# A planned instruction order in which the transfers of one in-order queue wait longer for what they depend on

## The chip, the core and the metric

The kernel runs on one core of one Trainium2 chip. A core has a matrix engine (PE), a vector engine (DVE), an activation engine (ACT), a general engine (POOL) and a synchronising engine (SP), which here issues every transfer. The metric is the device time of one execution in microseconds, as the median of several runs.

## What is computed

A pre-LayerNorm transformer block on 2048 rows of 640 values: multi-head attention with 32 heads of 20 values each, and then a gated feed-forward part without a nonlinearity. All tensors are bf16.

```python
def _A_ref(x, wqkv, wo):
    qkv = (x @ wqkv).reshape(B, S, 3, H, Dh).transpose(2, 0, 3, 1, 4)
    q, k, v = qkv[0], qkv[1], qkv[2]
    p = softmax(einsum("bhqd,bhkd->bhqk", q, k) * Dh ** -0.5)
    o = einsum("bhqk,bhkd->bhqd", p, v)
    return o.transpose(0, 2, 1, 3).reshape(B, S, D) @ wo

def _B_ref(x, w_gate, w_up, w_down):
    return ((x @ w_gate) * (x @ w_up)) @ w_down

h = x + _A_ref(layernorm(x), wqkv, wo)
out = h + _B_ref(layernorm(h), w_gate, w_up, w_down)
```

B is 1, S is 2048, D is 640, H is 32, Dh is 20, and the feed-forward width is 1728.

## The kernel before

**A planner writes the order.** The program is not a loop nest. While it is built, an event loop (lines 1587 to 1605) plays the kernel on an imagined chip: every operation has a planned duration (lines 68 to 81), a list of what it depends on and a key for its priority. Whenever an engine is free at the planned time, `try_start` (line 287) takes the ready operation of lowest key and emits its instruction. `finish` (line 241) is called with the planned end of an operation and makes those that depend on it available. What comes out is one fixed list of instructions for each engine. On the chip each engine works through its list in that order, and waits at an instruction until what it needs is there. A planned time is never seen by the chip, only the order that came of it. `SWITCH` (line 64) is the planned pause when PE goes from one way of tiling its array to another (line 502).

**The work.** The queries are cut into five chunks (line 37): three of 512 and two of 256. In each chunk the 32 heads form eight groups of four, so there are 40 groups in all, counted here from 0 to 39. A list `stream` (line 900) names the score blocks in order: chunk, group, head and key block. It has 2048 entries, and `spos` counts how far it is used. A group of the first three chunks has 64 entries, one of the last two has 32.

**Scores and exponentials.** PE writes scores into PSUM (`rows_into`, line 997, matmul at line 1013): three banks SA, two banks SB, and two banks D0 and D1. ACT takes the exponential of a whole SA or SB (line 1088) into the tiles EA or EB. Blocks in the D banks go to DVE, which makes integers that read as bf16 are an approximation of the exponential: line 1113 produces the first of four tiles Y, line 1123 two more on DVE, and line 1121 the fourth on POOL. PE then multiplies each tile by the values (line 1164), and accumulates in the bank ACC. The number of columns of VX includes ones, so that row 20 of each head in ACC is the softmax sum.

**Closing a group.** `close_group` (line 1180) is the chain that the change touches most. DVE copies ACC to SBUF (acs, line 1195). Then come small transfers on SP, all issued through `dma` (line 355, instruction at line 360): the sums go to DRAM (dscr<-acs), come back spread over partitions (dn<-dscr), DVE takes their reciprocal (rn, line 1199), which goes to DRAM (rscr<-rn), and comes back as a broadcast to 128 partitions (bc<-rscr, 256 KB for a chunk of 512 and 128 KB for one of 256). POOL multiplies (os, line 1227), and four or five transfers put the result in the layout of the output projection (ON<-os, line 1232). There are two acs tiles and one bc tile.

**What else is on SP's queue.** `dense` (line 574) projects q and k, and stores them in DRAM (qscr, kscr, line 586), from which they are loaded in the layout that the scores need (KTt, line 685; QT, line 700). There are also the loads of weights and x, the DMA transposes after a LayerNorm (line 477), and the stores of the output (line 887). SP is one queue: a transfer that is not ready holds all that stand behind it.

**Work beside attention.** The projections, the output projection, and the feed-forward part (jobs, `make_job`, line 524) are put by PE in between as it has time, in the D banks. When nothing is to be done and the planner thinks PE would be idle too long, it emits small filler matmuls (line 1472). What is left of the last chunks after attention runs at the end on PE.

Of the kernel before, what the change touches and what calls it, by code (L numbers as in the profile page):

```python
# [59 lines left out]
LAT = 0.12  # L60
LATP = 0.23
LPOOL = 0.1
DMA_LAT = 1.5
SWITCH = 0.105
WINDOW = 3.413


# [4 lines left out]
def c_psum(n):  # L72
    return 0.075 + 1.04e-3 * n
# [73 lines left out]
def kernel(  # L147
# [81 lines left out]
    now = [0.0]  # L229
    lockt = {"DVE": 0.0, "POOL": 0.0}  # L230

    def tick(t):
        heapq.heappush(wake, t)

    def enqueue(op):
        seq[0] += 1
        for e in op.engs:
            heapq.heappush(coming[e], (op.avail, seq[0], op))
        tick(op.avail)

    def finish(op, t, e=None, end=None):

        op.done = t
        for u in op.users:
            u.left -= 1
            if e == "DVE" and isinstance(u, Op) and u.engs == ("POOL",):
                u.avail = max(u.avail, t + LPOOL)
            u.avail = max(u.avail, end if e is not None and isinstance(u, Op) and u.engs == (e,) and e != "SP" else t)
            if u.left == 0:
                if isinstance(u, Op):  # L250
                    enqueue(u)
                else:
                    release_later(u.avail, u.cb)
        op.users = []
        tick(t)

    def add(engs, dur, fn, key, deps=(), **kw):
        if isinstance(engs, str):
            engs = (engs,)
        op = Op(engs, dur, fn, flat(key), deps, **kw)  # L260
        if op.left == 0:
            op.avail = max(op.avail, now[0])
            enqueue(op)
        return op
# [3 lines left out]
    def release_later(t, f):  # L268
        seq[0] += 1
        heapq.heappush(later, (t, seq[0], f))  # L270
        tick(t)

    def after(deps, cb):
        c = Call()
        c.left = 0
        c.avail = now[0]
        c.cb = cb
        for d in deps:
            if d.done is None:
                d.users.append(c)  # L280
                c.left += 1
            else:
                c.avail = max(c.avail, d.done)
        if c.left == 0:
            release_later(c.avail, cb)

    def try_start(e):
# [32 lines left out]
        if got.hook is not None:  # L320
            got.hook(t, end, e)
        got.fn(e)
        finish(got, end + got.lat, e, end)
        tick(end)
        return True


    def copy_on(e, o, i):
        if e == "ACT":
            nc.scalar.copy(o, i)  # L330
        else:
            nc.vector.tensor_copy(o, i)  # L332

    attn = {"started": False, "over": False}
# [20 lines left out]
    def dma(o, i, key, deps=(), dur=0.6, lat=1.25, kb=0):  # L355

        def hook(t, end, e):
            landed[0] = max(landed[0], end + 0.3) + kb / 310.0
            op.lat = max(lat, landed[0] - end + 1.4)
        op = add("SP", dur, lambda e: nc.sync.dma_start(o, i), key, deps, lat=lat, hook=hook)  # L360
        return op

    with tc.manual_schedule():
# [48 lines left out]
        def layer_norm(tiles, key, tdeps, dst_of, tr_key, on_pe, front=False, on_act=False):  # L412
# [37 lines left out]
            def one_done(end):  # L450
                left[0] -= 1
                if left[0] == 0:
                    finish(last, end + 0.3)
# [45 lines left out]
        def pe_issue(mode, grp, dur, w=0.25):  # L499
            t = max(now[0], pe["next"])  # L500
            if mode != pe["mode"]:
                t = max(t, pe["end"] + SWITCH)
                pe["mode"] = mode
# [20 lines left out]
        def make_job(mms, deps, evac, mode="C", front=False):  # L524

            j = Job(mms, list(deps), evac)
            j.out = Mark()
            j.mode = mode
            j.target = tgt[0]
            if front:  # L530
                j.target = -1e9
                jq.appendleft(j)
            else:
                jobs.append(j)
                jq.append(j)
            return j
# [5 lines left out]
        def both():  # L542
            return ("DVE", "ACT") if not attn["started"] or attn["over"] else ("DVE",)
# [30 lines left out]
        def dense(wname, col, w, b, dst):  # L574
            mms = []
            for c in range(KT):
                mms.append((lambda lo, hi, c=c: WQ[:, c, col + lo:col + hi],
                            lambda c=c: LT[:, c, b * 512:(b + 1) * 512], 0, 512, w, c == 0, c == KT - 1, 0.216))
            st = Mark()

            def evac(bank, pm):
                k = qd_n[0] % len(QD)
                qd_n[0] += 1
                deps = [pm] + ([qd_busy[k]] if qd_busy[k] is not None else [])
                ev = add(both(), c_psum(512), lambda e: copy_on(e, QD[k][0:w, :], bank[0:w, :]), EVK, deps)
                d = dma(dst, QD[k][0:w, :], 6, [ev], dur=0.75, kb=w, lat=2.2)
                qd_busy[k] = d
                after([d], lambda: finish(st, now[0]))
                return ev
            make_job(mms, [wl[wname], wl[wname + "0"]] + lt_ops, evac)  # L590
            return st
# [202 lines left out]
        def half_jobs(ci, half, pair, hsl, h_marks):  # L794
# [61 lines left out]
            for i, tt in enumerate(pair):  # L856
                ys = {}
                ym = [Mark(), Mark()]
                for hf in range(2):
# [6 lines left out]
                    def evac(bank, pm, tt=tt, hf=hf, ys=ys, ym=ym):  # L866
# [16 lines left out]
                        def rel():  # L883
                            finish(ym[hf], now[0])
                            if ym[1 - hf].done is not None:
                                row = q0 + tt * P
                                add("SP", 0.6, lambda e: nc.sync.dma_start(out2d[row:row + P, :], ys["t"][1][:]), 900, [],
                                    hook=stored, lat=DMA_LAT)
                        after([op], rel)
# [17 lines left out]
        spos = [0]  # L907
# [272 lines left out]
        def close_group(ci, g, end):  # L1180
# [50 lines left out]
            def out_of(p0, f, m):  # L1231
                return add("SP", 0.75, lambda e: nc.sync.dma_start(ON[f % P:f % P + m, on_of[ci, f // P], 0:cw], o[p0:p0 + m, 0:cw]),
                           (10,), mus, lat=DMA_LAT)
            os_use[k] = [out_of(*p_) for p_ in parts]
# [148 lines left out]
        def c_round(c, late, hold):  # L1383
# [4 lines left out]
            else:  # L1388
                t0 = max(now[0], pe["end"] + SWITCH)
                g = [t0] * 4  # L1390
# [93 lines left out]
        def dry():  # L1484

            return max(free["ACT"], now[0]) + sum(act_q.values())

        def room_for(d):

            t = max(now[0], pe["end"]) + d + (SWITCH if d or pe["mode"] != "R" else 0.0)  # L1490
            return t + SCORE + MARGIN <= dry()
# [145 lines left out]
```

The softmax here doesn't subtract the row's maximum and nothing guards it: scores larger than these inputs give would overflow.

## Time and profile before

| | us |
|---|---|
| median of 5 runs | 858.31 |
| lowest, highest | 853.0, 860.01 |
| the profiled execution: its own time | 858.31 |
| the profiled execution: span, first to last instruction | 856.5 |
| PE busy | 817.1 (95%) |
| ACT busy | 763.4 (89%) |
| DVE busy | 731.0 (85%) |
| POOL busy | 352.4 (41%) |
| mean granted TensorE clock | 0.991 of full speed |

"Busy" is the time in which at least one instruction of the engine runs. PE works on up to four parts of its array at once, so its share says little on how much more it could do. In a row of instructions, the name left of the arrow is written and the name right of it is read, with buffer numbers left out; the idle time in brackets is that of the engine just before the instruction, and after the arrow stands what ended it. SPq rows show the time that SP took to issue a transfer, not the transfer itself.

### The profile page before, as it was taken

What the parts mean: (1) busy time and instruction counts of PE and PEld (TensorE: products, weight loads), DVE (VectorE), ACT (ScalarE), POOL (GpSimd) and SP (SyncE); (2) the same over time, 40 slices, a digit from 0 to 9 for tenths busy, and PEclk for the clock granted to TensorE, in tenths of its full rate; (3) what the DMA queues carried; (4) which work ended last, traced back from release to release, by engine and by line L of the source; (5) the groups of instructions that cost most, each with busy time, mean ns of one, the idle gap of its engine ahead of it and who ended that gap; (6) DMA issues with size and microseconds to landing.
All of it is one profiled execution on the core that took longest, in us unless ns stands there. A gap on an engine that the chain in (4) does not pass through costs nothing. (4 is left out here: it accounts for less than half of the span.)

```text
span 856.5 us, 36007 instructions
## 1 busy us (share of the span) xinstructions
PE 817.1 (95%) x15355; PEld 403.8 (47%) x15355; DVE 731.0 (85%) x1961; ACT 763.4 (89%) x714; POOL 352.4 (41%) x593
## 2 busy tenths in 40 slices
PE   8999999999999999999999999999899999999998
PEld 3433343432333444444334444444555655555776
DVE  7888798887899899998999989898889998999342
ACT  5899899998989999999999999999989999999111
POOL 2034444453454444354554444444454444444100
PEclk9999999999999999999999999999999999999999
DMA  9603322322134412110101011100111111001200
GB/s 297 118 21 123 104 78 80 120 70 80 50 101 118 110 41 43 30 49 29 38 23 34 23 31 46 43 23 28 33 36 37 26 38 42 28 13 37 50 17 16
DMA packets 70545, 49.76 MB, mean 58 GB/s; under 512 B 31792, under 2 KB 66448, under 8 KB 70384
## 3 DMA queue, kind: packets, MB, share of 16 engines
q1 hardware_dynamic: 70384, 47.46, 20.3%
q8 instruction: 120, 1.97, 1.0%
q14 instruction: 41, 0.34, 0.1%
HBM read 30.88 MB, written 10.32 MB: 48 GB/s over the span
## 5 line engine op out<-in xcount | busy, mean ns | idle before, releaser
L1088 ACT ACTIVATE EA<-SA 128x1536 bf16<-128x1536 f32 x321 | 466.4, 1453 | 22.4 <-PE SA L1013 14.0
L1121 POOL TENSOR_SCALAR Y<-Y 128x512 uint16<-128x512 uint16 x452 | 290.5, 643 | 405.8 <-DVE Y L1123 262.5
L1113 DVE TENSOR_SCALAR Y<-D 128x512 uint16<-128x512 f32 x452 | 308.3, 685 | 50.6 <-PE SA L1013 18.6
L1088 ACT ACTIVATE EB<-SB 128x1024 bf16<-128x1024 f32 x319 | 328.7, 1030 | 8.1 <-PE SB L1013 4.8
L1164 PE MATMUL ACC<-Y,VX 128*32 128x512 bf16 (+1 forms) x2284 | 262.3, 340 | 5.6 <-DVE acs L1195 5.0
L1123 DVE TENSOR_SCALAR Y<-Y 128x512 uint16<-128x512 uint16 x904 | 242.8, 314 | 8.3 <-POOL Y L1121 0.5
L1164 PE MATMUL ACC<-EA,VX 128*32 128x512 bf16 (+1 forms) x1196 | 217.0, 341 | 0.0
L1013 PE MATMUL D<-QT,KTt 20*128 20x512 bf16 (+1 forms) x571 | 173.4, 339 | 8.8 <-DVE Y L1113 8.0
L1164 PE MATMUL ACC<-EB,VX 128*32 128x512 bf16 (+1 forms) x793 | 174.4, 342 | 0.0
L1013 PEld LDWEIGHTS <-KTt 20*128 20x128 bf16 x2560 | 72.0, 91 | 206.3 <-issue 197.3
L1347 PEld LDWEIGHTS <-R 128*32 128x32 bf16 x5370 | 123.7, 96 | 91.6 <-issue 74.0
L1164 PEld LDWEIGHTS <-VX 128*32 128x32 bf16 x4273 | 118.5, 96 | 87.1 <-issue 66.1
L1013 PE MATMUL SA<-QT,KTt 20*128 20x512 bf16 (+1 forms) x1196 | 129.5, 342 | 5.2 <-ACT EA L1088 4.0
L1347 PE MATMUL D<-L,R 128*32 128x256 bf16 x3240 | 128.0, 275 | 4.4 <-DVE HH L847 2.5
L1013 PE MATMUL SB<-QT,KTt 20*128 20x512 bf16 (+1 forms) x793 | 127.8, 343 | 1.1 <-ACT EB L1088 1.0
L1347 PE MATMUL D<-R 128*32 128x160 bf16 (+1 forms) x2130 | 106.8, 302 | 3.0 <-DVE KTt L332 0.9
L1227 POOL TENSOR_TENSOR os<-acs,bc 128x128 bf16<-128x128 f32 x128 | 57.1, 474 | 50.4 <-DMA bc<-rscr 30.7
L847 DVE TENSOR_TENSOR HH<-D,gs 128x256 bf16<-128x256 f32 (+1 forms) x103 | 43.6, 423 | 16.0 <-ACT gs L330 13.3
L1347 PE MATMUL D<-R,HH 128*32 128x320 bf16 x1120 | 55.5, 302 | 0.5 <-DVE Y L1113 0.4
L1347 PEld LDWEIGHTS <-HH 128*32 128x32 bf16 x1120 | 27.4, 96 | 20.3 <-issue 15.3
L332 DVE CAST gs<-D 128x256 bf16<-128x256 f32 x84 | 34.8, 415 | 1.5 <-PE D L1347 1.1
L1347 PE MATMUL D<-WO,ON 128*32 128x320 bf16 x560 | 32.4, 303 | 2.3 <-DVE hr L771 2.1
(78 smaller groups left out, 389.6 us busy)
## 6 DMA issues: line engine op xcount, KB each, us to landing
bc<-rscr SPq DMA_DIRECT2D x24, 256.0 KB
KTt<-kscr SPq DMA_DIRECT2D x6, 512.0 KB
QT<-qscr SPq DMA_DIRECT2D x22, 128.0 KB
t<-in_A_x_dram SPq DMA_DIRECT2D x16, 160.0 KB
bc<-rscr SPq DMA_DIRECT2D x16, 128.0 KB
R<-in_B_w_gate_dram SPq DMA_DIRECT2D x4, 480.0 KB
R<-in_B_w_up_dram SPq DMA_DIRECT2D x4, 480.0 KB
ON<-os SPq DMA_DIRECT2D x84, 20.0 KB
```

Of the source, the lines that this page charges most:

```text
L332: nc.vector.tensor_copy(o, i)
L847: mu = add("DVE", c_psum(256), lambda e: nc.vector.tensor_tensor(HH[0:M, f, :], bank[0:M, 256:512], GS[k][0:M, :], ALU.mult), EVK, mdeps)
L1013: nc.tensor.matmul(bank[:, n * cw:(n + 1) * cw], lhsT=KTt[32 * j:32 * j + Dh, g, kt * P:(kt + 1) * P], rhs=QTt[32 * j:32 * j + Dh, g, 0:cw ...
L1088: nc.scalar.activation(st["e"][eslot["i"]][:, 0:n * 512], src[:, 0:n * 512], ACT.Exp, scale=SCALE)
L1113: p_ = add("DVE", c_psum(512), lambda e: nc.vector.tensor_scalar(YT[ys[0]][:, :], bank, scalar1=EXP_A, scalar2=EXP_B, op0=ALU.mult, op1=AL ...
L1121: nc.gpsimd.tensor_scalar(o, i_, scalar1=float(d), scalar2=1.0, op0=ALU.add, op1=ALU.mult)
L1123: nc.vector.tensor_scalar(o, i_, scalar1=float(d), scalar2=None, op0=ALU.add)
L1164: nc.tensor.matmul(ACC[32 * j:32 * j + 32, 0:cw], lhsT=VX[:, kt, h * VS:h * VS + 32], rhs=ap, start=(n == 0), stop=last, tile_position=(0, ...
L1227: mus.append(add("POOL", 0.1 + 2.3e-3 * MUW, lambda e, c0=c0, c1=c1: nc.gpsimd.tensor_tensor(o[:, c0:c1], a[:, c0:c1], BC[0][:, c0:c1], AL ...
L1347: nc.tensor.matmul(bank[32 * j:32 * j + 32, c0:c1], lhsT=lhs(32 * j, 32 * j + 32), rhs=rhs(), start=first, stop=last, tile_position=(0, 32 ...
```

## The change

Three things are added to the planner, and one constant is changed. No instruction's operands or sizes are edited.

- When an operation ends, each SP transfer that depends on it becomes available later: by MSP (0.8 us) where it ended as a transfer of SP, otherwise by MSX (0.3 us). This holds from the start of attention until entry 1850 of 2048 of the stream (NEND), which lies in the second group of the last chunk.
- A store of projected q or k counts as done MQ (0.8 us) later for the loads that read it back.
- SWITCH goes from 0.105 to 0.1038.

```diff
@@ -60,8 +60,12 @@
 LAT = 0.12
 LATP = 0.23
 LPOOL = 0.1
+MSP = 0.8
+MSX = 0.3
+MQ = 0.8
+NEND = 1850
 DMA_LAT = 1.5
-SWITCH = 0.105
+SWITCH = 0.1038
 WINDOW = 3.413
@@ -238,11 +242,16 @@
+    def steady():
+        return attn["started"] and spos[0] < NEND
+
     def finish(op, t, e=None, end=None):
 
         op.done = t
         for u in op.users:
             u.left -= 1
+            if isinstance(u, Op) and u.engs == ("SP",) and steady():
+                u.avail = max(u.avail, t + (MSP if e == "SP" else MSX))
             if e == "DVE" and isinstance(u, Op) and u.engs == ("POOL",):
                 u.avail = max(u.avail, t + LPOOL)
@@ -585,7 +594,7 @@
                 d = dma(dst, QD[k][0:w, :], 6, [ev], dur=0.75, kb=w, lat=2.2)
                 qd_busy[k] = d
-                after([d], lambda: finish(st, now[0]))
+                after([d], lambda: finish(st, now[0] + MQ))
                 return ev
```

## The prediction

> **What bounds the kernel now.** I read the page first, then the engine waits, then the timelines of SP, DVE, PE and ACT around the longest ACT gaps, then busy time by stretch.
>
> ```profile
> PE 817.1 (95%) x15355; PEld 403.8 (47%) x15355; DVE 731.0 (85%) x1961; ACT 763.4 (89%) x714; POOL 352.4 (41%) x593
> L1088 ACT ACTIVATE EA<-SA 128x1536 bf16<-128x1536 f32 x321 | 466.4, 1453 | 22.4 <-PE SA L1013 14.0
> L1088 ACT ACTIVATE EB<-SB 128x1024 bf16<-128x1024 f32 x319 | 328.7, 1030 | 8.1 <-PE SB L1013 4.8
> ```
>
> From 19 to 791 us ACT runs one exponential after another: 466.4 + 328.7 = 795 us by start-to-end, less what overlaps. Back to back a pair EA, EB takes 2.24 us, so the stream paces attention, and an ACT gap is lost time. After 794 us comes a tail in which PE alone works (62 us). In the stretches from 60 to 790 us ACT is busy 704.3 of 730 us: 25.7 us of gaps. Whose are they?
>
> ```profile
> DVE rn L1199 <- DMA dn<-dscr: 7.8, 4, 2.8
> ...
> POOL os L1227 <- DMA bc<-rscr: 30.7, 17, 3.9
> ...
> PE D L1347 <- DMA L<-t: 0.8, 1, 0.8
> ```
>
> Total, number and longest: the reciprocal of the softmax sums (line 1199) is reached by DVE before its sums are back, four times, at 88, 205, 280 and 621 us. The last, followed over the engines (start, duration):
>
> ```profile
> 613.87 0.58 SPq L360 DMA_DIRECT2D bc<-rscr  x1
> 614.55 0.52 SPq L360 DMA_DIRECT2D dscr<-acs  x1
> 620.20 0.32 SPq L360 DMA_DIRECT2D dn<-dscr  x1
> ```
> ```profile
> 621.74 0.20 DVE L1199 RECIPROCAL rn<-dn 128x8 f32<-128x8 f32 x1 [2.81 <-DMA dn<-dscr]
> ```
> ```profile
> 622.56 0.26 PE L1013 MATMUL D<-QT,KTt 20*128 20x256 bf16 x1 [2.26 <-DVE Y L1113]
> ```
> ```profile
> 623.01 1.45 ACT L1088 ACTIVATE EA<-SA 128x1536 bf16<-128x1536 f32 x1 [2.40 <-PE SA L1013]
> ...
> 626.26 1.45 ACT L1088 ACTIVATE EA<-SA 128x1536 bf16<-128x1536 f32 x1 [0.87 <-PE SA L1013]
> ```
> ```profile
> 615.00:620.00 5.00, 4.98 (x126) 3.17 (x114) 3.93 (x12) 5.00 (x6) 1.23 (x2) 1.00 0.19 58
> 620.00:625.00 5.00, 2.74 (x47) 1.38 (x50) 3.26 (x9) 2.60 (x3) 4.28 (x8) 0.81 0.07 12
> 625.00:630.00 5.00, 4.75 (x130) 2.87 (x122) 4.03 (x12) 4.08 (x4) 3.28 (x6) 0.85 0.17 51
> ```
>
> dscr stood 0.1 us behind the 128 KB broadcast bc, so dn could only be issued 5.13 us after dscr's issue ended; DVE stood 2.81 us, the bank D it should have emptied held PE 2.26 us, ACT lost 2.40 + 0.87 us. The seventh column after the range is the granted TensorE clock: it falls to 0.81 and 0.85, the second bill of the same stall. The clock falls also near 91, 207 and 248 us: two of these three again just after such a reciprocal.
>
> **What the Trainium skill says.** "PSUM — Partial Sum Buffer", section "Engine vs sequencer instructions": "ScalarE/VectorE/GpSimdE queues are strict FIFO." The trace agrees: the 2.81 us held all that stood behind the reciprocal. "TensorE: Matmul & The Clock Gate", Part 1 on the clock gate: after an idle window of about 3.4 us the array runs at half clock for such a window. The half-clock stretches agree (about 3.4 us), the cause only in part: here 1.7 to 2.3 us of idle with thin work around it was enough. "DMA: Bandwidth & Descriptors", "Queues, rings and completion order": SP's transfers share one row of rings, consumed in ring order. The trace agrees: dscr to dn takes 1.2 us in quiet groups, and 5.13, 2.41 and 2.46 us where dscr stood 0.1 us behind bc. Same page, "Rules for kernel authors": issue early, wait late; this is what a margin in the plan does for the waiting engine.
>
> **The change part by part.** The profiled execution took 858.31 us (span 856.5 and 1.8 around it), which is also the median of the five runs; the sum is made against it. No operation's form is new; margins and SWITCH alter only when the planner believes things possible, hence the orders. I compared the two built orders. PE's first difference is at row 407, so nearly everything is reshuffled; the counts stay close.
>
> (1) Margins before the reciprocal. dscr's availability moves 0.3 us, dn's another 0.8, so the planner puts the reciprocal later among DVE's work. I summed the DVE work between the copy of line 1195 and the reciprocal in both orders (0.60 us for line 1113, 0.20 for line 1123, others by their rows): in groups 0 to 32 the mean cover rises from 5.7 to 6.9 us. In the four groups with waits, 1, 6, 9 and 24, it rises by 1.2, 1.6, 1.8 and 1.2 us against waits of 1.05, 2.61, 1.28 and 2.81. ACT's gaps after them, by its timeline, are 2.03, 3.31, 0.94 and 3.27: 9.55. Groups 1 and 9 are covered. Group 6 keeps 1.0 of 2.61, or 1.3 of ACT's 3.31. In group 24 bc no longer stands ahead of dscr; what comes in its place is in (6). Saved: 9.55 - 1.3 = 8.3. Bounds: 4 if the new order merely moves half of them, 9.6.
>
> (2) Margins before bc and the products. Between the copy and the os products (line 1227) POOL now has 9.4 instead of 7.5 of its line-1121 operations (mean, groups 0 to 33); at one per 770/452 = 1.7 us that is 3.1 us, against waits of 3.9 at most. Nearly all of the 30.7 us should go. POOL is busy 41%, so this is worth little: it delays a Y that PE wants. Taken 1; bounds 0 and 3 (the gaps of 2.2 us at 248, after a POOL backlog, and some more). SP's stores ON<-os wait 0.3 later in the plan and are queued behind fewer unready transfers; cover: the output projection wants them a chunk later, 0.
>
> (3) Transposes L<-t: 0.3 later; PE's wait of 0.76 cost ACT 1.19 at 654. Taken 0.5; 0 to 1.2.
>
> (4) Stores and loads of q and k through DRAM: 0.8 (MQ) and 0.3. Loads are planned one group or more ahead; that hides it, taken 0. Without that cover a late load would hold scores 1.1 us per load.
>
> (5) Counts. One EA of 1536 becomes 1024 wide and one EB of 512 (0.58) goes: 1.45 - 1.03 + 0.58 = 1.0 saved on ACT; DVE takes two more units, beside ACT. In the tail the change leaves the jobs the same, but the 112 filler matmuls between the projection and the down projection go (one before: 1.68 us on the chain), as three down projections now cover the last LayerNorm instead of one; likewise the 0.5 us wait for L. Saved 2.2 (bounds 0 and 2.8). The other 44 + 112 fillers more stand where the plan has idle PE: 0.
>
> (6) What it adds. In groups 24, 26, 27, 29, 30 and 33 bc of the previous group now stands between dscr and dn; before, only in 38. dn is then the small transfer behind the big one. Behind it wait rscr and the next stores on SP, and DVE at the reciprocal. Nearest row: dscr behind bc, 1.2 to 3.9 us late. Need without that: 0.1 + 0.54 (issue) + 1.2 (landing, which hides bc's 0.6) + 0.33 + 2.15 (dn's landing at 205 and 280 us) = 4.3 us; two transposes ahead in 27 and two loads in 30 add about 1.8 each. Cover: 7.0, 7.2, 6.8, 6.6, 6.4, 4.2. With 1.25 added, 27, 30 and 33 stand 0.5, 0.9 and 1.4 us short; group 34, without margins now (cover 5.6 to 4.6), too with bc ahead of dscr, perhaps 0.2. That is 3.0 us of DVE, times 3.27/2.81: 3.5. Low end 0.3; high end with 3.9 added: about 1.2, 1.0, 3.2, 1.6, 3.5 and 4.0 = 14.5, times 1.16 = 17.
>
> (7) SWITCH, 0.105 to 0.1038: each planned change of tiling mode ends 1.2 ns sooner; its cost is that another plan is drawn, with stalls of its own kind. About 16 us of ACT gaps are left outside (1); I let them grow by a sixth, 2.5. Bounds -3 and 6.
>
> Sum: -8.3 - 1.0 - 0.5 - 1.0 - 2.2 + 3.5 + 2.5 = -7.0; 858.3 - 7.0 = 851.3.
>
> **Rivals.** A, the above: 851.3, own range 846 to 854 (chance 0.50). B, stalls only move: the reshuffled plan has as many reciprocals early as before, at other places; only (5) counts: 858.3 - 3.2 = 855 to 858 (0.23). For it: waits come from coincidences on the queue, such as bc ahead of dscr. Against: cover rises in 32 of the first 33 groups. C, slower: dn behind bc lands 3.9 us late in all six groups, from about 600 us on: 851.3 - 3.5 + 17 = 865. It ends slower by over 0.5% once the lateness passes about 3.4 us; for it the 5.13 us at 614, against it the 2.4 us in two others of three (0.18). D, more than A: POOL and PE waits shrink with the rest, half of the remaining 16 us of gaps go too: about 842 (0.09). That the margins don't reach the order is excluded by the cover counted above.
>
> **How the numbers follow.** Half a per cent, 4.3 us, is about what a measurement of this kernel tells from no change. Faster: nearly all of A, and D: 0.57. Same: B and A's rim: 0.25. Slower: C: 0.18. The range 842 to 864 holds A, B, half of D and the near part of C, about 0.8.
>
> **What would show it.** (1) right: the row for rn waiting for dn falls from 7.8 to about 3 or less, with fewer half-clock stretches before 600 us. (2): os waiting for bc falls from 30.7 to under 10. (5): no 112 fillers at the tail, tail near 60 us. (6) or C: waits of rn for dn appear from 600 us on, with SP lines bc, dn adjacent. Wrong, if ACT's busy time from 60 to 790 us stays near 704 of 730 though those waits are gone: then PE's own pace made the gaps.

## The result, and the profile after

| | before | after |
|---|---|---|
| median of the runs taken side by side, us | 854.56 (80 runs) | 858.05 (43 runs) |
| ratio after / before, 95% interval | | 1.0033 [1.0019, 1.0047] |
| profiled execution: its own time; span | 858.31; 856.5 | 863.06; 861.3 |
| mean granted clock in that execution | 0.991 | 0.988 |

The change makes the kernel a third of a per cent slower. That is less than the half per cent that the prediction takes for no change, but the interval leaves out 1. One more run of the kernel after, 868.61 us at a mean granted clock of 0.982, counts as slow and is left out. The forecast of 851.3 us was not reached. The median of five runs on which it stood, 858.31, was itself 3.8 us above the median of 80, and the profiled execution after is 5.0 us above its median: both profiles show executions some 4 to 5 us longer than the median.

The page of the kernel after: busy time of the engines, and the two groups of exponentials (busy us, mean ns, then ACT's idle time ahead of them and what ended most of it).

```profile
PE 822.9 (96%) x15405; PEld 405.7 (47%) x15405; DVE 736.7 (86%) x1967; ACT 764.8 (89%) x713; POOL 354.2 (41%) x595
L1097 ACT ACTIVATE EA<-SA 128x1536 bf16<-128x1536 f32 x321 | 466.4, 1453 | 19.8 <-PE SA L1022 9.7
L1097 ACT ACTIVATE EB<-SB 128x1024 bf16<-128x1024 f32 x318 | 328.3, 1032 | 16.1 <-PE SB L1022 10.6
```

The work is nearly the same, but ACT's idle time ahead of exponentials rose from 22.4 + 8.1 = 30.5 us to 35.9. The waits of the kernel after (total, number, longest):

```profile
POOL os L1236 <- DMA bc<-rscr: 21.9, 12, 7.0
...
PE D L1356 <- DVE HH L856: 4.7, 9, 1.7
...
DVE rn L1208 <- DMA dn<-dscr: 2.0, 3, 0.9
...
PE SB L1022 <- DMA QT<-qscr: 1.6, 1, 1.6
```

The wait that the prediction counted most on did go, 7.8 to 2.0 us, and bc's fell from 30.7 to 21.9. The waits of SP's own queue at the stores ON<-os fell too, of which these are two rows before and two after:

```profile
SPq L1232 <- POOL os L1227: 77.9, 18, 7.7
...
SPq L1232 <- POOL Y L1121: 56.9, 13, 11.1
```
```profile
SPq L1241 <- POOL Y L1130: 57.8, 21, 9.6
...
SPq L1241 <- POOL os L1236: 31.5, 11, 7.7
```

So the waits that the change aims at are shorter. Where is the time? I summed ACT's gaps between the first and the last exponential over both timelines, by place (us; the first row is the five places that the prediction names, ahead of which a transfer was late):

| place in the span, us | before | after | difference |
|---|---|---|---|
| 87-97, 203-213, 278-286, 619-629, 652-658 | 11.09 | 1.37 | -9.7 |
| 471-485 | 0.15 | 5.26 | +5.1 |
| 246-260 | 2.22 | 4.46 | +2.2 |
| 629-652 | 0.04 | 2.29 | +2.3 |
| 60-87 | 0.48 | 1.81 | +1.3 |
| all the rest | 15.9 | 20.0 | +4.1 |
| sum | 29.9 | 35.2 | +5.3 |

The old gaps are nearly gone, and the gaps elsewhere grew by 15 us. The largest growth, followed over DVE, PE and ACT (start, duration, operation, in brackets the idle time ahead and what ended it):

```profile
469.74 2.12 DVE L1132 TENSOR_SCALAR Y<-Y 128x512 uint16<-128x512 uint16 x6
471.78 0.23 DVE L1208 RECIPROCAL rn<-dn 128x16 f32<-128x16 f32 x1
471.94 0.35 DVE L341 CAST gs<-D 128x256 bf16<-128x256 f32 x1
472.33 0.42 DVE L856 TENSOR_TENSOR HH<-D,gs 128x256 bf16<-128x256 f32 x1
```
```profile
472.81 0.51 PE L1356 MATMUL D<-L,R 128*32 128x256 bf16 x8 [1.73 <-DVE HH L856]
```
```profile
473.95 1.02 ACT L1097 ACTIVATE EB<-SB 128x1024 bf16<-128x1024 f32 x1 [1.60 <-PE SB L1022]
475.41 1.45 ACT L1097 ACTIVATE EA<-SA 128x1536 bf16<-128x1536 f32 x1 [0.44 <-PE D L1022]
478.30 1.02 ACT L1097 ACTIVATE EB<-SB 128x1024 bf16<-128x1024 f32 x1 [1.44 <-PE SB L1022]
```

The reciprocal has no bracket: its transfer was there. It stands instead, with a cast and a product of the feed-forward gate, behind six DVE operations that make tiles Y (line 1132). PE waits 1.73 us for the bank that the product empties; no engine in this chain waits for a transfer. After that the granted clock (seventh column after the range) is half, for 10.24 us in all (columns: length, then busy PE, PEld, DVE, ACT, POOL, clock, DMA share, GB/s):

```profile
470.00:473.00 3.00, 1.27 (x24) 0.45 (x18) 2.96 (x10) 2.35 (x3) 2.08 (x3) 0.99 0.03 5
473.00:476.00 3.00, 3.00 (x46) 1.19 (x42) 2.13 (x6) 1.61 (x2) 1.34 (x2) 0.50 0.10 32
476.00:479.00 3.00, 3.00 (x35) 0.79 (x27) 1.79 (x5) 1.56 (x2) 0.00 (x0) 0.50 0.14 56
```

PE is busy 3.00 of 3.00 us at half speed while ACT is busy about half: PE's pace makes the gaps here. Half clock for 10.24 us comes again from 247 us, after a PE wait of 0.98 us for the copy acs. The new stall at 75 us is at a transfer, the load of QT:

```profile
75.50 0.39 PE L1022 MATMUL SB<-QT,KTt 20*128 20x512 bf16 x2 [1.55 <-DMA QT<-qscr]
```

### The profile page after: what moved, and what is told of

Its sections match the earlier page's. It is cut to its first block, busy times and chain, and to the rows that moved or that the text cites. A ratio compares the mean times of both kernels' runs of the same rounds, so it can differ in the third digit from the quotient of the medians.

```text
span 861.3 us, 36116 instructions
## 1 busy us (share of the span) xinstructions
PE 822.9 (96%) x15405; PEld 405.7 (47%) x15405; DVE 736.7 (86%) x1967; ACT 764.8 (89%) x713; POOL 354.2 (41%) x595
## 4 chain that ended last, share of the span: by engine, by line
PE 62%; DVE 24%; ACT 5%; DMA 4%; issue 3%; SPq 1%; POOL 0%; DVEq 0%; POOLq 0%; ACTq 0%
PE D L1356 22%; PE ACC L1173 17%; DVE Y L1122 8%; PE SA L1022 7%; DVE Y L1132 6%; PE SB L1022 5%; PE D L1333 4%; PE D L1022 4%; ACT EA L1097 2%; ACT EB L1097 2%; DVE lst L445 2%; PE SB L1333 2%; DVE HH L856 1%; DVE gs L341 1%; DMA dn<-dscr 1%
## 5 line engine op out<-in xcount | busy, mean ns | idle before, releaser
L1173 PE MATMUL ACC<-Y,VX 128*32 128x512 bf16 (+1 forms) x2292 | 257.7, 341 | 4.2 <-DVE acs L1204 3.1
L1132 DVE TENSOR_SCALAR Y<-Y 128x512 uint16<-128x512 uint16 x908 | 248.7, 320 | 8.5 <-DVE Y L1122 0.5
L1173 PE MATMUL ACC<-EA,VX 128*32 128x512 bf16 (+1 forms) x1193 | 212.7, 343 | 0.0
L1173 PE MATMUL ACC<-EB,VX 128*32 128x512 bf16 (+1 forms) x794 | 176.3, 343 | 0.1
L1356 PEld LDWEIGHTS <-R 128*32 128x32 bf16 x5370 | 131.4, 96 | 95.1 <-issue 75.7
L1173 PEld LDWEIGHTS <-VX 128*32 128x32 bf16 x4279 | 115.9, 96 | 92.7 <-issue 72.3
L1356 PE MATMUL D<-L,R 128*32 128x256 bf16 x3240 | 132.3, 278 | 6.1 <-DVE HH L856 4.7
L1356 PE MATMUL D<-R 128*32 128x160 bf16 (+1 forms) x2130 | 109.6, 299 | 5.4 <-DVE VX L341 2.6
L1236 POOL TENSOR_TENSOR os<-acs,bc 128x128 bf16<-128x128 f32 x128 | 57.7, 478 | 35.1 <-DMA bc<-rscr 21.9
L856 DVE TENSOR_TENSOR HH<-D,gs 128x256 bf16<-128x256 f32 x104 | 44.0, 424 | 16.5 <-ACT gs L339 13.7
L339 ACT CAST gs<-D 128x256 bf16<-128x256 f32 (+1 forms) x20 | 7.4, 371 | 28.2 <-PE D L1333 16.5
```

The source lines that it names most:

```text
L856: mu = add("DVE", c_psum(256), lambda e: nc.vector.tensor_tensor(HH[0:M, f, :], bank[0:M, 256:512], GS[k][0:M, :], ALU.mult), EVK, mdeps)
L1132: nc.vector.tensor_scalar(o, i_, scalar1=float(d), scalar2=None, op0=ALU.add)
L1173: nc.tensor.matmul(ACC[32 * j:32 * j + 32, 0:cw], lhsT=VX[:, kt, h * VS:h * VS + 32], rhs=ap, start=(n == 0), stop=last, tile_position=(0, ...
L1236: mus.append(add("POOL", 0.1 + 2.3e-3 * MUW, lambda e, c0=c0, c1=c1: nc.gpsimd.tensor_tensor(o[:, c0:c1], a[:, c0:c1], BC[0][:, c0:c1], AL ...
L1356: nc.tensor.matmul(bank[32 * j:32 * j + 32, c0:c1], lhsT=lhs(32 * j, 32 * j + 32), rhs=rhs(), start=first, stop=last, tile_position=(0, 32 ...
```

## The experiments

A plan is here the instruction order that the planner makes, and a draw is one such plan: any edit of the planner gives another one, with stalls that nobody chose. My theory after the result (theory 1 in the expectations) was: margins and SWITCH each draw another plan; a plan has some ten stalls of its own whatever the margins are, and what a plan costs by chance is as large as what the margins save. Rival one (theory 3): margins help by themselves, and the SWITCH drawn with them spoilt it. Rival two (theory 2): a later reciprocal is itself harmful, since everything behind it, the broadcast and the products on POOL, gets later. All ratios are to the kernel before, run beside it, with 95% intervals.

**The two parts apart.** Margins alone:

```diff
-SWITCH = 0.1038
+SWITCH = 0.105
```

> The three margins with SWITCH back at 0.105. Theory 1 (the margins do take the early reciprocals away, but that is worth little, and another plan brings stalls of its own): between 0.995 and 1.006 of the kernel before, with at most 3 us of DVE waiting for dn<-dscr. Theory 2 (the margins cost time by themselves, later bc and os): 1.005 or more. Theory 3 (the margins gain what the prediction said, and 0.1038 drew a bad plan): 0.993 or less.

SWITCH alone, no margins:

```diff
-SWITCH = 0.105
+SWITCH = 0.1038
```

> No margins, SWITCH 0.1038. Theory 1: between 0.995 and 1.006, with 5 us or more of DVE waiting for dn<-dscr. Theory 2: 0.998 or less. Theory 3: 1.010 or more.

Measured: margins alone 0.9961 [0.9946, 0.9976], SWITCH alone 0.9973 [0.9959, 0.9988]. Each part alone is slightly faster, both together slower: 0.9973 x 1.0060 = 1.0033, so on top of the new SWITCH the same margins cost 0.60%. Rival one wanted 0.993 or less for the margins alone; a gain of that size isn't there. The waits of the kernel with SWITCH alone:

```profile
POOL os L1227 <- DMA bc<-rscr: 9.0, 8, 2.5
...
DVE rn L1199 <- DMA dn<-dscr: 1.9, 3, 0.8
```

Without any margin, these waits are no longer than in the kernel after (21.9 and 2.0). My theory had expected 5 us or more of waiting for dn here, and missed. That the two waits fell from before to after is then no proof of the margins: another draw alone does as much to waits that were bad in the first.

**More draws, with and without margins.** If margins are worth something, they must be so over several plans. SWITCH was set to four more values, each with and without them; in the diff 0.1045 stands for 0.106, 0.103 and 0.1039 too, and without margins the line before is 0.105.

```diff
-SWITCH = 0.1038
+SWITCH = 0.1045
```

> No margins, SWITCH 0.1045: one more plan of the same kind, to see how far plans differ that nothing was meant to change. Theory 1: it differs from the kernel before by as much as the change did, some 0.2 to 0.7% in either direction. Theories 2 and 3: within 0.2%.

> The three margins, SWITCH 0.1045: the pair of the run without margins at the same SWITCH. Theory 1: within 0.6% of that run in either direction. Theory 2: slower than that run by 0.4% or more. Theory 3: faster than it by 0.7% or more.

> No margins, SWITCH 0.106: a fourth plan without margins. If the plan that is drawn sets the time: anywhere between 0.993 and 1.006 of the kernel before, with a DVE wait for dn<-dscr of 2 to 8 us.

> The margins at SWITCH 0.106. So far the margins changed the time by -0.4, -0.3 and +0.6% at the same SWITCH. If that is a small gain under a larger scatter: within -1.0 to +0.6% of the run without margins at 0.106, with a DVE wait for dn<-dscr of 2 us or less. If the margins cost time in some plans by a mechanism of their own: 0.5% or more slower.

> No margins, SWITCH 0.103: a fifth plan without margins. If the drawn plan sets the time: between 0.993 and 1.006 of the kernel before.

> The margins at SWITCH 0.103: the fifth pair. The four pairs so far changed by -0.4, +0.6, -0.3 and 0.0%. If the margins are worth nothing on average: within 0.7% of the run without margins at 0.103 in either direction. If they are worth what the prediction said: 0.6% faster or more.

> The changed kernel with SWITCH 0.1039 for 0.1038. As for MSX 0.302: 1.002 to 1.005 if it is the margins, most likely 0.993 to 1.000 if it is the plan.

> No margins, SWITCH 0.1039: the sixth pair. If plans without margins scatter as so far: 0.994 to 1.001 of the kernel before; the margins at the same SWITCH within 0.7% of it.

Measured, with the three waits in us (the reciprocal for dn; POOL's products for bc; SP at the stores for POOL):

| SWITCH | no margins: ratio | waits | margins: ratio | waits | margins / none |
|---|---|---|---|---|---|
| 0.105 | 1 (before) | 7.8; 30.7; 139 | 0.9961 [0.9946, 0.9976] | 1.4; 18.1; 70 | -0.39% |
| 0.1038 | 0.9973 [0.9959, 0.9988] | 1.9; 9.0; 129 | 1.0033 [1.0019, 1.0047] (after) | 2.0; 21.9; 89 | +0.60% |
| 0.1045 | 0.9946 [0.9930, 0.9962] | 4.5; 14.5; 121 | 0.9914 [0.9890, 0.9938] | 1.0; 4.8; 77 | -0.32% |
| 0.106 | 0.9994 [0.9977, 1.0012] | 3.2; 24.3; 134 | 0.9998 [0.9974, 1.0022] | 1.0; 6.5; 93 | +0.04% |
| 0.103 | 0.9988 [0.9963, 1.0014] | 2.0; 22.0; 137 | 0.9958 [0.9937, 0.9979] | 1.4; 13.7; 114 | -0.30% |
| 0.1039 | 0.9997 [0.9974, 1.0020] | 2.9; 16.0; 125 | 0.9978 [0.9960, 0.9996] | 1.6; 18.2; 93 | -0.19% |
| mean | 0.9983 | 3.7; 19.4; 131 | 0.9974 | 1.4; 13.9; 89 | -0.09% |

What follows: the margins do what they are for. From the copy acs to the point where DVE is ready for the reciprocal, the mean over groups 0 to 32 is 6.2 to 6.4 us in the six profiles without margins and 7.5 to 8.2 us in the six with them. The waits they aim at get shorter, on average 3.7 to 1.4, 19.4 to 13.9 and 131 to 89 us. The time follows by -0.09% on average, with a standard error of 0.15% from the spread of the six (0.37%), so no effect is shown. ACT's idle time ahead of exponentials, in the one profile of each, is 28.3 us on average without margins and 27.6 with them. Four of the six pairs are below zero, one is at +0.04%. A gain of some 0.3% in most plans can't be excluded either; the six pairs don't settle it. Six settings of a constant that is only a planned pause spread by 0.54% without margins and by 1.2% with them. Nor do the listed waits rank the plans: SWITCH alone at 0.1038 has 1.9 and 9.0 us of waits and 0.9973; 0.103 with margins has 1.4 and 13.7 and 0.9958.

The plan at 0.1045 with margins is the best of all, 849.67 us (six runs) against 857.10 for the kernel before beside it, and beats both kernels. Its page shows it where ACT waits:

```profile
L1097 ACT ACTIVATE EA<-SA 128x1536 bf16<-128x1536 f32 x321 | 466.3, 1453 | 11.3 <-PE SB L1022 3.5
L1097 ACT ACTIVATE EB<-SB 128x1024 bf16<-128x1024 f32 x319 | 329.2, 1032 | 9.2 <-PE SB L1022 4.1
```

Idle ahead of exponentials is 20.5 us against 30.5 before and 35.9 after. It is the best of twelve draws, and its ratio is flattered by that choice.

**One more small step.** The kernel after with a margin 0.002 us longer, which is another draw near it:

```diff
-MSX = 0.3
+MSX = 0.302
```

> The changed kernel with MSX 0.302 for 0.300. If the margins cost something at this SWITCH: within 0.15% of the changed kernel, 1.002 to 1.005 of the kernel before. If the changed kernel is one bad plan of many: another one, most likely 0.993 to 1.000.

Measured: 1.0016 [0.9994, 1.0039], not told apart from 1 or from the kernel after. Its timeline has the gaps at 248 and 473 us as the kernel after has (1.70 and 1.28 us). The kernel with margins at SWITCH 0.1039, with 0.9978, has neither of the two. This fits with those stalls being what makes the draw with margins at 0.1038 a bad one; one of each is not enough to show it.

**The plan kept, one thing moved.** To take the draw out of the comparison, the planner was left as before, and only the order in which instructions are written out was changed on one engine. First, each reciprocal waits until four more DVE instructions are out, its store rscr<-rn with it; PE, ACT and POOL keep their order, and SP's moves by one place at most. Then the same with up to eight (6.6 on average; there the store rscr moves by up to three places).

```diff
+            kept.append(rec)
...
+        for rec in list(kept):
+            rec["n"] -= 1
+            if rec["n"] <= 0:
+                let_go(rec)
...
-        got.fn(e)
+        if e == "DVE":
+            emit_dve(got)
+        else:
+            got.fn(e)
```

> The plan of the kernel before, kept as it is on PE, ACT and POOL, with each reciprocal of the softmax sums moved back by four DVE instructions (about 1.4 us) after planning, its store behind it: step (1) of the prediction without another plan. If the early reciprocals cost what step (1) says: the DVE wait for dn<-dscr falls from 7.8 to 3 us or less and the ratio to the kernel before is 0.990 to 0.994. If those waits are only a place where time passes that would be lost anyway: the wait falls as much, and the ratio is 0.998 to 1.002.

> As the kept plan with the reciprocals four instructions later, but up to eight (mean 6.6, about 2.3 us; bc<-rscr is not moved and limits it). If step (1) is right: the DVE wait for dn<-dscr under 1 us and 0.988 to 0.993. If four took all there is to take: the same ratio as that run. If later reciprocals hurt what waits for bc: more POOL waits for bc<-rscr than the 30.7 us of the kernel before, and a higher ratio than with four.

Measured: 1.0049 [1.0028, 1.0070] and 1.0122 [1.0078, 1.0165]. The waits with four, then with eight:

```profile
POOL os L1264 <- DMA bc<-rscr: 54.1, 25, 5.2
...
DVE rn L1225 <- DMA dn<-dscr: 1.6, 2, 1.0
```
```profile
POOL os L1264 <- DMA bc<-rscr: 82.9, 25, 11.7
...
DVE rn L1225 <- DMA dn<-dscr: 1.2, 1, 1.2
```

The wait for dn goes as wanted, 7.8 to 1.6 to 1.2 us. The chain behind it gets later, bc is issued later, and POOL now stands at the products for 54 and 83 us instead of 31. POOL's Y, which PE needs, and the stores stand behind that. The same wait is removed, and the time goes up, which neither expectation for the first of the two allowed. With eight the profile shows the loss: ACT's idle time ahead of exponentials is 37.7 us, against 30.5 before. With four it is 30.2 us, in an execution of 858.76 us, 2.9 below the median of its kernel: that the time rose is shown there by the runs, and where it went is not. So rival two holds for the kept plan in the time; the longer wait of POOL as its cause is the likely one, not a separate test.

Would it help to move the products along? First they alone were moved: two POOL operations later in 32 of the 40 groups (less in the others), the stores behind them; then both, reciprocals by four and products by two. It is the edit above, with this on POOL:

```diff
+    KP = 2
...
+                    pool_kept.append(rec)
...
+        elif e == "POOL":
+            emit_pool(got)
```

> The plan of the kernel before, kept on PE, ACT and DVE, with the four or two products os of each group moved back by two of POOL's other operations (about 3.4 us), their stores behind them: step (2) alone. The reciprocals stay where they were. If what POOL waits for bc is what costs (the two kept plans with later reciprocals lengthened it by 23 and 52 us and lost 3 and 10 us at full clock): POOL waits fall from 30.7 to 8 us or less and the ratio to the kernel before is 0.992 to 0.996. If it is worth what the prediction said (1 us): 0.998 to 1.000. If the wait of DVE for dn is what costs: 1.000, as that wait stays near 7.8 us.

> Both moves in the kept plan: reciprocals four DVE instructions later, os two POOL operations later; this is what the margins do to the chain, without another plan. If both waits cost what the prediction said: 0.989 to 0.992. If only the POOL wait costs: it falls to 15 us or less and the ratio is 0.995 to 0.999. If neither is worth anything: 0.999 to 1.002.

Measured: 1.0353 [1.0301, 1.0404] and 1.0213 [1.0168, 1.0259], slower than anything that was expected. With the products alone moved, the wait for bc is all but gone, and the one for dn is 3.6 times as long as before:

```profile
DVE rn L1270 <- DMA dn<-dscr: 28.3, 16, 4.7
...
POOL os L1311 <- DMA bc<-rscr: 6.2, 6, 2.1
```

Why is seen on SP's timeline at 148 to 165 us, with the kernel before at the same place below it:

```profile
147.48 0.41 SPq L420 DMA_DIRECT2D R<-in_B_w_down_dram  x1
156.05 1.33 SPq L1318 DMA_DIRECT2D ON<-os  x2
157.43 0.73 SPq L420 DMA_DIRECT2D kscr<-HH  x1
158.21 2.25 SPq L1318 DMA_DIRECT2D ON<-os  x3
160.56 0.71 SPq L420 DMA_DIRECT2D kscr<-L  x1
161.38 0.53 SPq L420 DMA_DIRECT2D dscr<-acs  x1
...
164.40 0.38 SPq L420 DMA_DIRECT2D dn<-dscr  x1
```
```profile
145.50 1.32 SPq L1232 DMA_DIRECT2D ON<-os  x2
146.88 0.73 SPq L360 DMA_DIRECT2D kscr<-HH  x1
147.65 2.25 SPq L1232 DMA_DIRECT2D ON<-os  x3
150.01 0.71 SPq L360 DMA_DIRECT2D kscr<-L  x1
150.82 0.53 SPq L360 DMA_DIRECT2D dscr<-acs  x1
```

What came of it on DVE, PE and ACT:

```profile
169.67 0.25 DVE L1270 RECIPROCAL rn<-dn 128x16 f32<-128x16 f32 x1 [4.66 <-DMA dn<-dscr]
```
```profile
170.95 0.59 PE L1434 MATMUL D<-R 128*32 128x160 bf16 x12 [4.59 <-DVE VX L392]
```
```profile
172.18 1.02 ACT L1150 ACTIVATE EB<-SB 128x1024 bf16<-128x1024 f32 x1 [4.36 <-PE D L1075]
```

SP stands at the first store for eight microseconds, until the products of the group before are done (156.02). The copy acs of the next group ended at 156.75, but dscr is issued only at 161.38, 4.6 us later, behind five stores. In the kernel before the first store at this place is issued at 145.50, 4.6 us before the copy ends (150.07), dscr follows the copy by 0.75 us, and the reciprocal hardly waits (0.07 us). In all, SP stands at the stores for POOL for 223 us (139 before), and ACT 59.4 us ahead of exponentials (30.5 before). With both moved, what the margins were to do to this chain, the waits are 9.7 us for dn and 16.2 for bc, SP's at the stores 198, and ACT's idle time 44.8.

Last, the other way round: on SP alone, each store ON<-os goes behind the next transfer of another kind.

```diff
+    KS = 1
...
+            sp_kept.append([KS, op.fn])
...
+        if e == "SP":
+            emit_sp(got)
```

> The plan of the kernel before, kept on PE, ACT, DVE and POOL; on SP each store ON<-os goes behind the next transfer of another kind, as the margins often put it behind QT<-qscr. If SP's standing at these stores (139 us in the kernel before) holds transfers that are wanted: that wait falls to 100 us or less and the ratio is 0.994 to 0.998. If what stands behind them is not wanted that soon: 0.999 to 1.002. If the transfer now ahead is itself late: 1.003 or more.

Measured: 1.0158 [1.0116, 1.0199]. SP waits only 33.4 us at stores for POOL, the least of all. The reciprocal waits 17.8 us instead of 7.8, and ACT stands idle 38.8 us ahead of exponentials; once, at 211 us, the reciprocal waits 4.51 us, when the last store stood behind a load of QT and dscr behind both: 6.3 us from the copy to dscr, 3.6 in the kernel before. Taking the wait from the head of the queue put it at other transfers.

## Why the prediction was wrong

The margins moved the chain as foreseen, and the waits fell; the time did not follow. The step that failed is (7), the price of another plan. That 858.05 us lies in the stated range of 842 to 864 is no merit: the range was wide enough for two of the rivals. Point by point:

- **(1) and (3), the reciprocal and the transposes: the gain was there, at its places.** 8.3 + 0.5 us were forecast; the gaps at the five places shrank by 9.7. The size is right in part by luck: it isn't a saving of the margins alone. SWITCH alone takes the wait for dn to 1.9 us, and six plans without margins have 3.7 on average. The 7.8 us priced as a fault of the kernel were in good part that of one draw. And in the kept plan a later reciprocal by itself loses 0.5%.
- **(7), another plan is drawn: this is the step that failed.** It let the gaps "outside (1)" grow "by a sixth, 2.5", with bounds -3 and 6. They grew by 9.7 + 5.3 = 15 us in the profiled execution, where (6) and (7) together had 6.0. That execution is a bad one: it lies 5 us above the median, with two half-clock stretches of 10.24 us, and the kernel with MSX 0.302 has the gap at 473 without such a stretch. Still, 9.7 us of gain and a median that rose by 3.5 leave some 13 us that the new plan costs, if the old gaps cost other executions as much as the profiled one; (7) had 2.5. Twelve draws, from 0.9914 to 1.0033, spread by 1.2%, 10 us: the term should have had bounds as wide as the whole sum, and would have left nothing to forecast but no change.
- **(2), the products: priced at 1 us of gain, with the stores at 0.** The wait was to fall under 10 us and fell to 21.9, and no gain shows. The cover for the stores, "the output projection wants them a chunk later, 0", overlooked that the cost of a late store isn't the late data: in an in-order queue it is dscr and dn behind it. Moving products or stores alone cost 3.5% and 1.6%. In the kernel after, where SP's waits at the stores fell, this term did no visible harm; only the kept plan shows it.
- **(4), loads of q and k: "planned one group or more ahead; that hides it" failed once.** QT was late at 75 us: PE 1.55 us, ACT 1.22. SWITCH alone shows such a gap too (0.97 at 76), so it isn't MQ's doing alone.
- **(5), counts and tail: half right.** The filler matmuls went, and the tail from the last copy acs fell from 61.32 to 59.73 us: 1.6 of the 2.2 forecast. The wait for L stayed, 0.58 us at 832.79. ACT has one instruction fewer, but no 1.0 us came of it: the stream less its gaps became 1.4 us longer. Neighbouring exponentials overlap by about 0.12 us (1.453 + 1.030 - 2.24 for a pair, halved), and each of some 20 gaps more loses that: the overlaps sum to 55.0 us before and 53.1 after.
- **(6) and rival C: the kind was right, the price near, the places mostly not.** A wait for dn of 0.88 us came at 664 us, in group 27, with bc between dscr and dn as foreseen. Groups 30, 33 and 34 have none; the other long one, 0.95 us at 808 us, is in group 39. With one of 0.16 us at 88 us that is 2.0 us of DVE in three places, against 3.0 taken, in part by luck; C's 3.9 us in each of six groups didn't happen.
- **Rival B, stalls only move, 855 to 858, came closest in the time.** Its reason was half wrong: the reciprocals were not as early as before. The stalls moved to other instructions, at other engines. The prediction's own test for being wrong held: ACT's busy time from 60 to 790 us is 699.7 of 730 us, 704.3 before, though the old waits are gone.
- **A reading of the profile before:** "1.7 to 2.3 us of idle" ahead of half clock leaves out two of the four places. PE's longest idle times there are 1.20, 1.74, 1.49 and 2.26 us.

**What stays open.** Which of the new stalls belong to margins and which to chance isn't told apart plan by plan; nor is it settled why one plan has 20 us of gaps and the next 35, since the listed waits don't rank them. Whether margins are worth some 0.3% in a typical plan would take more pairs. Moved to full clock as in the last section, five of the six pairs are faster with margins and the mean is -1.5 us with a standard error of 0.8: a hint, no proof.

## What to carry to other kernels

In an order that a planner writes, a stall seen in the trace belongs to that one order: an edit that redraws the order removes it and draws others, so its length is no saving until several draws with and without the edit have been compared. A wait on an in-order queue must be priced by what stands behind it: all five moves in the kept plan lost time, 0.5 to 3.5%, and each of the four that aimed at one wait shortened it and lengthened another; moving reciprocal and products together did not cure it. Judge such an edit by the gaps of the engine that paces the stage, summed by place, and not by the wait it aims at.

## What the runs showed of the hardware

- **The times of one kernel go with its mean granted clock.** Over the 43 runs of the kernel after, the two correlate by -0.91: 853.0 to 853.8 us at a clock of 1.0, 862.3 to 863.1 at 0.988. The slope is about 7.5 us for each 0.01 of clock, or some 1.5 us more for each half-clock stretch of 3.41 us (an estimate from this slope). A stall can lengthen a run and bring the half clock as well, so not all of this need be the clock's doing. Moved to full clock with that slope, before is 851.8 us (its 57 runs beside the first experiments), after 854.3, margins at SWITCH 0.1045 848.3; the order of these three is the same.
- **Half-clock stretches came after PE had stood idle for only 1 to 2.3 us at a time.** Not every such idle time brought one: the 1.55 us at 75 us in the kernel after did not, nor the 1.73 us near 472 us with MSX 0.302. They lasted 3.41 us in the profile before, and 10.24 us twice in the profile after, where PE was busy without a break at half clock for most of it. The Trainium skill, "TensorE: Matmul & The Clock Gate", Part 1 on the clock gate, has at least one idle window of about 3.4 us ahead of half clock, and full clock again after one busy window of that length. The idle was shorter here, and the busy time before full clock came back was longer in the two stretches of the profile after.
- **A small transfer landed late behind large ones.** At 164 us in the kernel with moved products, dn (issued at 164.40, used at 169.67, DVE waiting) had two loads of KTt (512 KB each) issued just ahead of it and took 5.3 us. At the same place in the kernel before, behind the same two loads, it took at most 4.6 us (153.84 to 158.41). At 205 and 280 us of the kernel before, without them and with DVE waiting too, it took 2.5. That the loads are the cause is likely from the order of issue, and not tested.
